# Linear attention and tanh-shrink MLP on one core: w_out's third quarter ahead of v, kv of batch 1 three slots later, first tiles of chunk 1 by head pairs

## The chip, the cores and the metric

The kernel runs on one core of one Trainium2 chip. The metric is device time in microseconds (us), the median of several executions. The kernel before takes 295.09 us (three runs, 294.81 to 295.49). The times of a kernel differ between chips and between executions by some tenths of a microsecond.

## The reference

```python
q_p, k_p = phi(q), phi(k)                    # phi(x) = exp(x) if x <= 0, else x + 1; 8 batches, 8 heads, 576 x 64
kv  = einsum('bhsd,bhse->bhde', k_p, v)
z   = sum(k_p, axis=2)
num = einsum('bhsd,bhde->bhse', q_p, kv)
den = einsum('bhsd,bhd->bhs', q_p, z)[..., None] + 1e-06
x   = (num / den) as [4608 tokens, 512]      # heads side by side
h   = x @ w_in                               # 512 -> 2048
out = (h - tanh(h)) @ w_out                  # 2048 -> 512
```

## The kernel before

The tokens are worked off in nine chunks of 512. Each chunk has a first layer of 16 tiles of four matmuls (one for each pair of heads; line 366), a tanh on ScalarE (372), a subtraction on VectorE into gT (373), and a second layer of 64 matmuls (387) in 16 slots of four. The attention of the later batches is tucked in between: lists s1 (behind tiles of the first layer) and s2 (behind slots of the second) say what is issued where. In the timelines here each engine takes its instructions in program order, so these lists also fix the order on VectorE and ScalarE.

In chunk 0 the second layer runs by quarters of w_out: slots 0 to 3 use the first quarter, 4 to 7 the second, 8 to 11 the third, 12 to 15 the fourth. Batch 1 is prepared there:

```python
def a_kv(b, banks):      # kv and z of a batch, masked into kz by VectorE (L177, L186)
def a_den(b, banks):     # denominators (L276), + 1e-6 (L281), reciprocal (L285)
def num1():              # numerators (L317, L320), copied out of PSUM by ScalarE (L344, L346)
def a_split(b):          # the reciprocal as a sum of bf16 numbers, w (L295 to L298)
def spread1(h):          # w spread over the partitions by matmuls (L354), two scales into xT (L359)

load_v(1)                # before: v of batch 1, then the third and fourth quarter of w_out
load_wo(2)
load_wo(3)
...
s2[7].append(lambda: (a_qT_pe(1, 0, side), a_qT_pe(1, 1, side), a_kv(1, side)))
s2[8].append(lambda: b0_scale_rest(side))
s2[9].append(lambda: a_den(1, side))
s2[10].append(lambda: (num1(), a_split(1)))
s2[11].append(lambda: spread1(0))
s2[12].append(lambda: q2(0))                    # exp and ramp of the first half of q of batch 2
s2[13].append(lambda: (spread1(1), q2(1)))      # exp and ramp of the second half
s2[14].append(lambda: q2(2))                    # both minima, then the transpose by DMA
s2[15].append(lambda: a_kphi(2, 0))
```

phi of a half batch is three instructions: exp on ScalarE (L134), the ramp max(x, 0) + 1 on VectorE (L135), and the minimum of both on VectorE (L136).

From batch 2 on the reciprocals take another way: from VectorE to DRAM (ds, L305), and back as a broadcast to all partitions (rdb, L308). Numerator products (L328) read rdb and free the two PSUM banks in which the numerators are made in turn. The loads of the batch after next are issued when the transposed q of the next batch is there:

```python
s1[0].append(lambda: (gate(qT_t[n1]), load_k(n2), load_q(n2), load_v(n2)))
s1[10 if c == 1 else 8].append(lambda: (a_den(n1, attn), a_spread(n1)))
...
if c == 1:
    s1[1].append(lambda: a_kphi(2, 1))
    for i in range(2):
        s1[3].append(lambda i=i: a_vp(2, i))    # v of batch 2 copied beside its column of ones, VectorE, L189
```

## Time and profile before

| engine | busy us | share of 293.2 us |
|---|---|---|
| TensorE | 285.2 | 97% |
| VectorE | 174.6 | 60% |
| ScalarE | 139.6 | 48% |

The main lines are shown in the prediction below. This is VectorE's timeline of the kernel before, around the start of chunk 1 (start, duration, engine, line, operation, sizes, number, and in brackets the idle time before it and what ended it):

```profile
51.02 0.45 DVE L135 TENSOR_SCALAR r<-qraw 128x1152 bf16<-128x1152 bf16 x1
51.39 1.42 DVE L136 TENSOR_TENSOR qp<-e,r 128x1152 bf16<-128x1152 bf16 x2
...
54.73 1.23 DVE L373 TENSOR_TENSOR gT<-ps_all,th 128x1024 bf16<-128x1024 f32 x1 [0.15 <-ACT th L372]
...
57.10 1.22 DVE L373 TENSOR_TENSOR gT<-ps_all,th 128x1024 bf16<-128x1024 f32 x1
58.23 0.82 DVE L189 COPY vp<-v 128x1152 bf16<-128x1152 bf16 x2
```

VectorE is nearly full here. In 51 to 62 us it is busy for 10.10 of 11 us, although it is busy for only 60% of the whole span.

### The profile page before, as it was taken

How to read it: one execution, taken by the hardware profiler on the slowest of the kernel's cores; microseconds unless marked ns; L12 is line 12 of the kernel's file. 1: busy time of each engine (PE TensorE's matmuls, PEld its weight loads, DVE VectorE, ACT ScalarE, POOL GpSimd, SP SyncE). 2: the span in 40 equal slices, each digit the busy share in tenths (PEclk: the TensorE clock that was granted, in tenths of full speed). 3: DMA queues.
4: the chain of work that ended last, by engine and by line, in shares of the span. 5: the costliest groups of instructions: out<-in, count | busy, mean ns of one | idle time of the engine just before them, and what ended most of it. 6: DMA issues, size and time to landing. Idle time of an engine off the chain costs nothing.

```text
span 293.2 us, 4504 instructions
## 1 busy us (share of the span) xinstructions
PE 285.2 (97%) x1801; PEld 134.3 (46%) x1801; DVE 174.6 (60%) x265; ACT 139.6 (48%) x168; POOL 33.3 (11%) x55
## 2 busy tenths in 40 slices
PE   8899999999999999999999999999999999999994
PEld 2544453454444444444444445444444444444443
DVE  4759857887567764786478646865581456106600
ACT  4938536947344643455246524661552155126411
POOL 8673030030030003000300020000000000000000
PEclk9999999999999999999999999999999999999999
DMA  6999999998999758955895669667117310131032
GB/s 101 194 204 212 208 207 216 200 145 153 234 163 185 160 118 139 218 117 129 136 223 127 139 134 183 134 154 143 38 24 178 73 36 0 38 84 24 0 74 72
DMA packets 39077, 38.94 MB, mean 133 GB/s; under 512 B 16336, under 2 KB 33808, under 8 KB 38288
## 3 DMA queue, kind: packets, MB, share of 16 engines
q0 software_dynamic: 17552, 18.35, 38.6%
q1 hardware_dynamic: 21344, 20.17, 30.3%
q8 instruction: 14, 0.23, 0.3%
q10 hardware_dynamic: 160, 0.13, 0.1%
q14 instruction: 7, 0.06, 0.1%
HBM read 43.91 MB, written 9.55 MB: 182 GB/s over the span
## 4 chain that ended last, share of the span: by engine, by line
PE 79%; DMA 11%; issue 7%; POOL 2%; DVE 0%; ACT 0%; POOLq 0%
PE ps_all L387 37%; PE ps_all L366 36%; DMA qraw<-in_q_dram 6%; DMA w_in_sb<-in_moe_w_in_dram 3%; PE ps_all L199 2%; DMA kraw<-in_k_dram 2%; PE ps_all L317 2%; PE ps_all L604 1%; PE ps_all L276 1%; POOL qraw L90 0%; ACT e L134 0%; POOL kraw L93 0%; DVE qp L136 0%; POOL v L93 0%; POOL w_out_sb L115 0%
## 5 line engine op out<-in xcount | busy, mean ns | idle before, releaser
L366 PE MATMUL ps_all<-xT,w_in_sb 128*128 128x512 bf16 x576 | 128.0, 379 | 0.3 <-DVE xT L244 0.3
L387 PE MATMUL ps_all<-w_out_sb,gT 128*128 128x512 bf16 x560 | 127.8, 379 | 0.0
L373 DVE TENSOR_TENSOR gT<-ps_all,th 128x1024 bf16<-128x1024 f32 x64 | 77.9, 1218 | 59.8 <-ACT th L372 59.8
L372 ACT ACTIVATE th<-ps_all 128x1024 f32<-128x1024 f32 x64 | 65.5, 1024 | 57.0 <-PE ps_all L366 47.1
L366 PEld LDWEIGHTS <-w_in_sb 128*128 128x128 bf16 x576 | 55.3, 98 | 66.6 <-issue 0.6
L387 PEld LDWEIGHTS <-gT 128*128 128x128 bf16 x560 | 54.1, 98 | 64.3 <-issue 0.3
L396 ACT COPY osb<-ps_all 128x512 f32<-128x512 f32 (+1 forms) x36 | 20.9, 583 | 73.4 <-PE ps_all L387 54.2
L328 DVE TENSOR_TENSOR xT<-ps_all,rdb 128x512 bf16<-128x512 f32 x24 | 16.3, 689 | 13.4 <-PE ps_all L317 11.2
L134 ACT ACTIVATE e<-qraw 128x1152 bf16<-128x1152 bf16 x16 | 18.5, 1162 | 6.9 <-DMA qraw<-in_q_dram 6.9
L134 ACT ACTIVATE e<-kraw 128x1152 bf16<-128x1152 bf16 x15 | 17.5, 1166 | 0.2 <-DMA kraw<-in_k_dram 0.2
L136 DVE TENSOR_TENSOR qp<-e,r 128x1152 bf16<-128x1152 bf16 x16 | 12.0, 757 | 7.8 <-ACT e L134 7.2
L136 DVE TENSOR_TENSOR kp<-e,r 128x1152 bf16<-128x1152 bf16 x15 | 11.4, 759 | 8.3 <-ACT e L134 7.5
L383 POOL COPY g<-qT 1x1 bf16<-1x1 bf16 x5 | 1.2, 240 | 120.6 <-DMA qT<-qp 120.6
L378 DVE TENSOR_TENSOR gT<-ps_all,th 128x512 bf16<-128x512 f32 x16 | 10.3, 685 | 2.4 <-ACT th L377 1.7
L377 ACT ACTIVATE th<-ps_all 128x512 f32<-128x512 f32 x16 | 9.2, 598 | 4.3 <-PE ps_all L366 3.1
L317 PE MATMUL ps_all<-qT,kz 128*128 128x512 bf16 x28 | 10.1, 379 | 0.0
L444 PE MATMUL ps_all<-zero 128*128 128x512 bf16 x29 | 8.8, 463 | 1.2 <-DVE zero L405 1.2
L135 DVE TENSOR_SCALAR r<-qraw 128x1152 bf16<-128x1152 bf16 x16 | 7.3, 453 | 2.2 <-DMA qraw<-in_q_dram 2.2
L199 PE MATMUL ps_all<-vp,kp 64*128 64x136 bf16 x216 | 7.4, 220 | 0.4 <-POOL g L383 0.4
L199 PEld LDWEIGHTS <-kp 64*128 64x128 bf16 x216 | 6.4, 94 | 3.0 <-issue 2.1
L285 DVE RECIPROCAL rden<-den 128x144 f32<-128x144 f32 x7 | 7.4, 1053 | 0.2
L394 DVE COPY osb<-ps_all 128x128 f32<-128x128 f32 x1 | 0.3, 292 | 11.6 <-PE ps_all L604 11.6
(82 smaller groups left out, 121.7 us busy)
## 6 DMA issues: line engine op xcount, KB each, us to landing
out_dram<-osb SPq DMA_DIRECT2D x70, 128.0 KB
rdb<-ds SPq DMA_DIRECT2D x12, 576.0 KB
kraw<-in_k_dram POOLq DMA_DIRECT2D x7, 576.0 KB, 7.1
qraw<-in_q_dram POOLq DMA_DIRECT2D x7, 576.0 KB, 9.0
v<-in_v_dram POOLq DMA_DIRECT2D x7, 576.0 KB, 12.2
w_out_sb<-in_moe_w_out_dram POOLq DMA_DIRECT2D x4, 512.0 KB, 16.4
w_in_sb<-in_moe_w_in_dram POOLq DMA_DIRECT2D x6, 256.0 KB, 8.6
qraw<-in_q_dram POOLq DMA_DIRECT2D x2, 288.0 KB, 4.6
```

The lines of the kernel that those rows point to most:

```text
L134: return (lambda: nc.scalar.activation(e, x, AF.Exp), lambda: nc.vector.tensor_scalar(r, x, 0.0, 1.0, ALU.max, ALU.add), lambda: nc.vector ...
L136: lambda: nc.vector.tensor_tensor(y, e, r, ALU.min))
L199: nc.tensor.matmul(ps[hg][:, i, :], kp[r, i, j].rearrange("p h d -> p (h d)"), vp[r, i, j, :], start=(j == 0), stop=(j == J - 1))
L317: nc.tensor.matmul(ps, kz[:, p // 2, p % 2, 0:128], qT[:, p % 2, 0:8, p // 2, :], start=True, stop=True)
L328: nc.vector.tensor_mul(xT[:, p, S * b:S * b + 512].rearrange("p (j t c) -> p j t c", j=8, t=4), ps.rearrange("p j (t c) -> p j t c", t=4), ...
L366: nc.tensor.matmul(h, w_in_sb[:, 2 * (p % 2) + p // 2, fi * 128:(fi + 1) * 128], xT[:, p, c * 512:(c + 1) * 512], start=(n == 0), stop=(n ...
L372: nc.scalar.activation(th, h, AF.Tanh)
L373: nc.vector.tensor_sub(gT[:, fi:fi + 2, :], h, th)
L377: nc.scalar.activation(th, h, AF.Tanh)
L378: nc.vector.tensor_sub(gT[:, fi, :], h, th)
L387: nc.tensor.matmul(o, gT[:, fi, i * 128:(i + 1) * 128], w_out_sb[:, fi, :], start=(fi == 0), stop=(fi == NF - 1))
L396: nc.scalar.copy(osb[:, f0:f1], o[:, f0:f1])
```

## The change

The intent is to close three holes of TensorE, 2.1 us together. The transposes of batch 1 are pulled apart, so that the second pass need not wait for its q; kv goes to slot 10, and everything behind it follows closely; w_out's third quarter is loaded ahead of v, because its slot now comes before kv. The second spread ends up behind slot 15, directly ahead of chunk 1, so the first two tiles of chunk 1 take the pairs of heads that are ready first. phi of batch 2 is rearranged, and kv of batch 2 moves one tile back.

```diff
+    load_wo(2)
     load_v(1)
-    load_wo(2)
     load_wo(3)
...
-            s2[7].append(lambda: (a_qT_pe(1, 0, side), a_qT_pe(1, 1, side), a_kv(1, side)))
-            s2[8].append(lambda: b0_scale_rest(side))
-            s2[9].append(lambda: a_den(1, side))
-            s2[10].append(lambda: (num1(), a_split(1)))
-            s2[11].append(lambda: spread1(0))
... (q2 and its slots 12 to 15)
+            s2[7].append(lambda: a_qT_pe(1, 0, side))
+            s2[8].append(lambda: a_qT_pe(1, 1, side))
+            s2[10].append(lambda: (a_kv(1, side), b0_scale_rest(side)))
+            s2[11].append(lambda: (a_den(1, side), num1(), a_split(1)))
+            s2[13].append(lambda: spread1(0))
...
+            s2[12].append(lambda: exp2(qs, q_t, qp_t, "qp", 0))
+            s2[13].append(lambda: exp2(qs, q_t, qp_t, "qp", 1))
+            s2[14].append(lambda: exp2(ks, k_t, kp_t, "kp", 0))
+            s2[15].append(lambda: (spread1(1), rest2(qs[0]), rest2(qs[1]), a_qT_dma(2), rest2(ks[0])))
...
-            s1[7 if c == 1 else 5].append(lambda: a_kv_cols(n1, attn))
+            s1[8 if c == 1 else 5].append(lambda: a_kv_cols(n1, attn))
...
+            if c == 1 and fi == 1:
+                for two in (0, 2):
+                    for f, o in ((0, ps_all[:, dense.order[(dense.n - 2) % 6], :]), (1, h)):
+                        for p in (two, two + 1):
+                            l1mm(c, f, o, p, p)
+            elif c != 1 or fi > 1:
+                for p in range(NP):
+                    l1mm(c, fi, h, p, p)
```

exp2 issues the exp of a half, rest2 its ramp and its minimum.

More of the change, by code (lines that the diff above doesn't have):

```diff
@@ L525, with exp2, rest2 @@
             s2[0].append(prepare)
-            s2[7].append(lambda: (a_qT_pe(1, 0, side), a_qT_pe(1, 1, side), a_kv(1, side)))
-            s2[8].append(lambda: b0_scale_rest(side))
-            s2[9].append(lambda: a_den(1, side))
-            s2[10].append(lambda: (num1(), a_split(1)))
-            s2[11].append(lambda: spread1(0))
-            def q2(n):
-                if n == 0:
-                    sub["q"] = [phi_pieces(2, q_t, qp_t, "qp", i) for i in range(2)]
-                if n < 2:
-                    for f in sub["q"][n][:2]:
-                        f()
-                else:
-                    for x in sub["q"]:
-                        x[2]()
-                    a_qT_dma(2)
-            s2[12].append(lambda: q2(0))
-            s2[13].append(lambda: (spread1(1), q2(1)))
-            s2[14].append(lambda: q2(2))
-            s2[15].append(lambda: a_kphi(2, 0))
+            s2[7].append(lambda: a_qT_pe(1, 0, side))
[3 more added lines that the diff above has]
+            s2[13].append(lambda: spread1(0))
+            qs, ks = [], []
+            def exp2(pieces, src, store, name, i):
+                pieces.append(phi_pieces(2, src, store, name, i))
+                pieces[i][0]()
+            def rest2(f):
+                f[1]()
+                f[2]()
+            s2[12].append(lambda: exp2(qs, q_t, qp_t, "qp", 0))
+            s2[13].append(lambda: exp2(qs, q_t, qp_t, "qp", 1))
+            s2[14].append(lambda: exp2(ks, k_t, kp_t, "kp", 0))
+            s2[15].append(lambda: (spread1(1), rest2(qs[0]), rest2(qs[1]), a_qT_dma(2), rest2(ks[0])))
         elif n1 < B:
-            s1[7 if c == 1 else 5].append(lambda: a_kv_cols(n1, attn))
+            s1[8 if c == 1 else 5].append(lambda: a_kv_cols(n1, attn))
             s1[10 if c == 1 else 8].append(lambda: (a_den(n1, attn), a_spread(n1)))
@@ L553 @@
             s1[1].append(lambda: a_kphi(2, 1))
-            for i in range(2):
-                s1[3].append(lambda i=i: a_vp(2, i))
+            s1[3].append(lambda: (a_vp(2, 0), a_vp(2, 1)))
         if c >= 1 and n2 < B:
@@ L582 @@
             h = first() if c == 0 else dense()
-            for p in range(NP):
-                l1mm(c, fi, h, p, p)
+            if c == 1 and fi == 1:
[6 more added lines that the diff above has]
+                    l1mm(c, fi, h, p, p)
             if c == 0:
```

## The prediction

> **What bounds the kernel now.** I read the page's busy rows first, then the chain that ended last in order of time, then TensorE's timeline, and last the timelines of the other engines over 30 to 80 us.
>
> ```profile
> PE 285.2 (97%) x1801; PEld 134.3 (46%) x1801; DVE 174.6 (60%) x265; ACT 139.6 (48%) x168; POOL 33.3 (11%) x55
> DMA  6999999998999758955895669667117310131032
> ```
>
> TensorE is busy in 97% of the span, and the DMA row is full for the first third: the loads are the second limit there.
>
> ```profile
> 234.05 13.81 PE ps_all L366 x64
> 247.87 13.81 PE ps_all L387 x64
> ```
>
> The chain gives the rate of a full stream: 64 matmuls in 13.81 us, 0.2158 us each. From 80 us on TensorE's rows follow one another at this rate without gaps. So only lost time in the first chunk and around the first two stages can be won. TensorE's timeline shows it:
>
> ```profile
> 31.03 7.07 PE L387 MATMUL ps_all<-w_out_sb,gT 128*128 128x512 bf16 x32
> 37.94 0.68 PE L164 MATMUL ps_all<-ident,qp 128*128 128x128 bf16 x9
> 39.17 0.68 PE L164 MATMUL ps_all<-ident,qp 128*128 128x128 bf16 x9 [0.56 <-DVE qp L136]
> 39.78 1.66 PE L177 MATMUL ps_all<-v,kp 64*128 64x192 bf16 x36
> ...
> 47.26 0.31 PE L354 MATMUL ps_all<-w,sel 32*128 32x144 bf16 x8 [0.69 <-ACT ns L344]
> ...
> 51.30 7.07 PE L366 MATMUL ps_all<-xT,w_in_sb 128*128 128x512 bf16 x32
> 58.74 1.24 PE L199 MATMUL ps_all<-vp,kp 64*128 64x136 bf16 x36 [0.37 <-POOL g L383]
> ```
>
> There are three holes. Counted in starts (the previous start plus its matmuls times 0.2158) they are 0.7 us before the second transposes, which wait for qp of batch 1; 0.86 us before the first spread (the four L387 from 45.54 end at 46.40); and 0.53 us before the kv of batch 2 (51.30 + 32 x 0.2158 = 58.21). The last is put down to POOL, but VectorE's copies of v into vp ran from 58.23 to 59.05: VectorE is the real releaser. Together that is 2.1 us, 0.7% of the span. It is all that the change could win.
>
> **What the Trainium skill says.** "TensorE: Matmul & The Clock Gate", Back-to-back issue gap: an isolated gap of N/2.4 + 2.5 ns, 215.8 ns for 512 columns, and a sustained 131 ns. The trace shows 215.8 ns in full streams, so I count with that; 131 ns does not show here. "Perfetto Trace Analysis", Identifying Performance Opportunities: an optimization looks for gaps on the most contended engine and for what ends them, and the limiting engine can change over time. The trace agrees: TensorE limits from 80 us, VectorE has hardly a gap from 51 to 61 us. "PSUM — Partial Sum Buffer", the section on bank collisions: guard by bank, not address. That is why the spread waits for ScalarE's copies out of banks 4 to 7. "DMA: Bandwidth & Descriptors", Queues, rings and completion order: each DMA engine takes turns between queue rows by packets. The four small ds writes issued at 65.45 to 66.74 nevertheless let rdb start only at 70.65, when the v load of batch 3 landed (60.32 + 10.3); other chunks need about 1 us.
>
> **The change part by part.** It removes no arithmetic. By the order of instructions each engine has the same ones, in another order.
>
> *Loads.* Landing is issue plus landing time: q of batch 1 at 19.39 + 16.5 = 35.9, v at 22.28 + 16.5 = 38.8, third quarter of w_out at 23.01 + 18.3 = 41.3, fourth at 43.9. So w_out costs 2.5 us and v 2.9 us of a full DMA. Swapped: w_out 38.4, v 41.3, fourth as before.
>
> *TensorE to the end of chunk 0.* Slot 7 ends at 37.94 as before. Nine transposes, 0.5: 38.44; the w_out quarter lands just then (0 to 0.2 lost). Slot 8: 39.36. The second qp is ready at 39.11, so the second transposes do not wait: 39.86. Slots 9 and 10: 41.59, v is there. kv 1.59: 43.18; rest numerators 0.12 and slot 11: 44.16. VectorE makes kz until 43.18 + 1.06 = 44.24, so den starts at about 44.3 and num ends at 45.63. Slots 12 and 13: 47.36. w comes 2.74 + 0.48 us after den's start, as from 43.32 to 46.54 now: 47.52. So the spread starts at 47.6, and 0.86 lost becomes 0.2. Slots 14 and 15: second spread at 49.66, chunk 1 at 49.89 instead of 51.30: **1.4 us won so far**.
>
> *Chunk 1's first tiles.* The four matmuls of pairs 0 and 1 fill 0.86 us, to 50.75. VectorE's scales start 0.35 after the spread and take 0.67 and 0.75: pair 2 is ready at about 50.75, pair 3 at 51.45. So pair 3 costs 0.5 us; without the new order it would cost about 0.9.
>
> *VectorE pays next.* In the kernel before it did one ramp of q in its wait for the spread; now all four scales come first, then q, q, k. Starts are 0.55 from ramp to minimum and 0.68 on from it (29.13, 29.68, 30.36 in its timeline). From 51.35 three pairs take 3.69: the first subtraction of chunk 1 starts at 55.04 and ends at about 56.2 (before: 54.73). Its bank pair is needed by the seventh tile at 52.15 + 4 x 0.863 = 55.6: 0.6 lost. One more pair (1.23) puts the second subtraction at 57.42 to 58.65 (before it started at 57.10); the ninth tile wants that bank at 57.97: 0.7 lost. That tile ends at 59.56, vp is ready at 59.4, kv follows at 59.56 and ends at 60.73. The tenth tile starts at 60.73; now it starts at 59.91 + 0.863 = 60.77. The sum of the won 1.4 and the lost 0.5 + 0.6 + 0.7, with the 0.53 vp wait absorbed: **-0.05 us at this point**.
>
> *DMA.* The transpose of q of batch 2 now follows all eight output writes and the second minimum: 53.9 instead of 53.48. Its landing (58.27 now, 4.8 after) gates the loads of batch 3, whose end released ds and rdb:
>
> ```profile
> 79.10 1.29 DVE L328 TENSOR_TENSOR xT<-ps_all,rdb 128x512 bf16<-128x512 f32 x2 [2.26 <-DMA rdb<-ds]
> ```
>
> The third numerator of chunk 1, at 79.98, needs the bank that this line's first product frees at about 79.78: slack is only 0.2 us. If rdb comes 0.4 later, TensorE loses 0.2; TensorE could not pass this point more than 0.2 earlier unless rdb also came earlier. No such wait shows in later chunks.
>
> So the estimate is max(-0.05, 0.4 - 0.2) with the transpose perhaps a little quicker without writes behind it: about 0.0 to +0.2 us on the span.
>
> **Rivals.** (a) *The 1.4 us is kept.* For it: later chunks have slack, and VectorE is busy only 60% overall. Against it: VectorE's lack of gaps at 51 to 61 us and the rdb line. It would give about 293.7; half kept, 294.4. (b) *The loads bind.* Both new landings are within 0.3 us of need. If the w_out quarter or v came 0.7 us late, everything after it would slide: 295.8. (c) *The transpose, loads, ds, rdb chain slides by a us.* The DMA queues are full at 62 to 69 us: 295.9. (d) *A clock difference.* The granted clock is 0.998, and nothing in the change adds work: excluded.
>
> **Range and chances.** The median of 295.09 plus 0.0 to 0.2 gives 295.1. The low side is rival (a) half kept plus run spread (0.3 below the median), 294.2; the high side is (b) or (c), 295.9. Two per cent is 5.9 us; all holes together are 2.1, so faster by 2% is excluded by the working, and slower needs a stall of 6 us that nothing suggests.
>
> **What would show it.** The second transposes start without a wait near 39.4; the first spread near 47.6, waiting for w; chunk 1's first matmul near 49.9; waits of TensorE for VectorE in the first, seventh and ninth tiles of chunk 1, together 1.5 to 2 us; kv of batch 2 near 59.5; the first product with rdb near 79.1 to 79.5. I am wrong if the scales or ramps end earlier than I say (then more is kept), if the seventh and ninth tiles do not wait, if L387 waits for w_out near 38.4 by more than 0.3 us, or if rdb lands before 78.5.

## The result, and the profile after

The changed kernel took 295.5 us (median of four, 295.45 to 295.57) against 294.95 for the kernel before (four, 294.7 to 295.49; three of them are the runs named at the top). The ratio is 1.0016, with a 95% interval of 0.9999 to 1.0034: the same, since differences under 2% are called the same here. A ratio is the mean time of one kernel's runs over that of the other's, so it is not quite the ratio of the medians. A second job gave 295.16 against 295.06, ratio 1.0004 (0.9985 to 1.0024).

The page of the kernel after, the busy row and the DMA row:

```profile
PE 283.4 (96%) x1773; PEld 133.9 (46%) x1801; DVE 174.6 (59%) x265; ACT 139.4 (47%) x168; POOL 33.4 (11%) x55
DMA  6999999878989658945796669767107310131032
```

The lower busy time of TensorE is not real: 28 of 1801 matmul records are missing in this trace. Among the rows of chunk 1 below none is missing: 5 + 19 + 8 + 4 matmuls are nine tiles of four.

TensorE's timeline of the kernel after, from slot 7 of chunk 0:

```profile
38.19 0.67 PE L164 MATMUL ps_all<-ident,qp 128*128 128x128 bf16 x9
...
39.56 0.67 PE L164 MATMUL ps_all<-ident,qp 128*128 128x128 bf16 x9
...
47.85 0.30 PE L354 MATMUL ps_all<-w,sel 32*128 32x144 bf16 x8
...
50.15 1.30 PE L366 MATMUL ps_all<-xT,w_in_sb 128*128 128x512 bf16 x5
51.74 4.26 PE L366 MATMUL ps_all<-xT,w_in_sb 128*128 128x512 bf16 x19 [0.29 <-DVE xT L359]
56.58 1.89 PE L366 MATMUL ps_all<-xT,w_in_sb 128*128 128x512 bf16 x8 [0.57 <-DVE gT L373]
58.94 1.02 PE L366 MATMUL ps_all<-xT,w_in_sb 128*128 128x512 bf16 x4 [0.48 <-DVE gT L373]
59.90 1.24 PE L199 MATMUL ps_all<-vp,kp 64*128 64x136 bf16 x36
```

The three holes are closed but for 0.20 us at the first spread (45.92 + 8 x 0.2158 = 47.65, and it starts at 47.85), and three new ones are open. The first transposes already stand 0.25 us later than before (38.19 against 37.94). In eleven more profiles, in which TensorE has the same instructions up to there, they stood between 37.74 and 38.46, and the second profile of this same kernel has the 37.74. That is the spread of the opening, and I subtract it from here on. Chunk 1 starts at 50.15 instead of 51.30: 1.15 us earlier, 1.4 without the opening. Then TensorE waits for the fourth scale, at the seventh tile for the first subtraction and at the ninth for the second. Counted in starts, with 0.2158 us for a matmul, that is 51.74 - (50.15 + 5 x 0.2158) = 0.51, 56.58 - (51.74 + 19 x 0.2158) = 0.74 and 58.94 - (56.58 + 8 x 0.2158) = 0.63. Together 1.88 us were given back. The tenth tile starts when kv with its 1.17 us is through, at 59.90 + 1.17 = 61.07, which is 22.88 us after the first transposes; before it was 60.77, or 22.83.

VectorE's timeline of the kernel after shows who asked for it back:

```profile
50.27 1.42 DVE L359 TENSOR_TENSOR xT<-ns,ps_all 128x576 bf16<-128x576 f32 x2 [0.58 <-PE ps_all L354]
51.61 0.46 DVE L135 TENSOR_SCALAR r<-qraw 128x1152 bf16<-128x1152 bf16 x1
52.17 0.76 DVE L136 TENSOR_TENSOR qp<-e,r 128x1152 bf16<-128x1152 bf16 x1
...
55.31 1.22 DVE L373 TENSOR_TENSOR gT<-ps_all,th 128x1024 bf16<-128x1024 f32 x1
...
57.67 1.22 DVE L373 TENSOR_TENSOR gT<-ps_all,th 128x1024 bf16<-128x1024 f32 x1
```

After the second scale it sits idle for 0.58 us, and then has no gap that the view lists until the second subtraction. The subtractions come at 55.31 and 57.67 instead of 54.73 and 57.10, so tiles that are ready earlier find their banks still taken.

The second wall comes later. The chain that ended last, of the kernel after, in order of time (start, duration, what), has both:

```profile
55.39 1.15 DVE gT L373
...
66.75 4.31 DMA ds<-rden
...
71.71 7.90 DMA rdb<-ds
...
79.73 0.70 DVE xT L328
80.44 0.04 issue
80.48 0.38 PE ps_all L317
```

It runs through VectorE at the start of chunk 1, then through ds and rdb, and enters TensorE at the third numerator, at 80.48. This is TensorE's timeline of the kernel before at the same place:

```profile
78.95 1.03 PE L387 MATMUL ps_all<-w_out_sb,gT 128*128 128x512 bf16 x4
79.85 0.38 PE L317 MATMUL ps_all<-qT,kz 128*128 128x512 bf16 x1
```

The difference of 0.63 us (80.48 against 79.85) stays to the end: the last chunk's tail stands at 286.32 instead of 285.69. Without the opening it is 0.38 us; in the second profile of the changed kernel it is 0.24 (42.15 against 41.91 in the table below).

### The profile page after: what moved, and what is told of

It reads as the page before. It is cut to its first block, busy times and chain, and to the rows that moved or that the text cites. A ratio compares the mean times of both kernels' runs of the same rounds, so it can differ in the third digit from the quotient of the medians. Undisturbed runs are those within 1.5% of the kernel's fastest.

```text
span 293.8 us, 4475 instructions
## 1 busy us (share of the span) xinstructions
PE 283.4 (96%) x1773; PEld 133.9 (46%) x1801; DVE 174.6 (59%) x265; ACT 139.4 (47%) x168; POOL 33.4 (11%) x55
## 4 chain that ended last, share of the span: by engine, by line
PE 80%; DMA 9%; DVE 5%; ACT 2%; issue 1%; POOL 1%; SPq 1%; DVEq 0%; ACTq 0%; POOLq 0%
PE ps_all L366 37%; PE ps_all L387 35%; DMA rdb<-ds 3%; DMA v<-in_v_dram 2%; DMA out_dram<-osb 2%; PE ps_all L199 2%; PE ps_all L317 2%; DMA ds<-rden 1%; PE ps_all L276 1%; DVE gT L378 1%; DVE gT L373 1%; ACT th L377 1%; ACT osb L396 1%; PE ps_all L177 1%; DVE qp L136 1%
## 5 line engine op out<-in xcount | busy, mean ns | idle before, releaser
L387 PE MATMUL ps_all<-w_out_sb,gT 128*128 128x512 bf16 x547 | 126.0, 379 | 0.7
L328 DVE TENSOR_TENSOR xT<-ps_all,rdb 128x512 bf16<-128x512 f32 x24 | 16.3, 690 | 13.8 <-PE ps_all L317 11.2
```

The costliest lines, as they stand in the source:

```text
L328: nc.vector.tensor_mul(xT[:, p, S * b:S * b + 512].rearrange("p (j t c) -> p j t c", j=8, t=4), ps.rearrange("p j (t c) -> p j t c", t=4), ...
L387: nc.tensor.matmul(o, gT[:, fi, i * 128:(i + 1) * 128], w_out_sb[:, fi, :], start=(fi == 0), stop=(fi == NF - 1))
```

## The experiments

Times are from five rounds unless said otherwise. All experiments gave correct results. A kernel's runs are compared with the runs of the kernel before that the record lists with them; e5 to e10 and the second job ran on one chip and share eleven of these, e1 to e4 ran on another. The table has, from each profile, the start of the tenth tile of chunk 1, the start of the third numerator of chunk 1 and the end of the span, all counted from the first transposes of chunk 0 (us).

| kernel | median us | before, listed with it | ratio (95%) | tenth tile | third numerator | end |
|---|---|---|---|---|---|---|
| before | 295.09 | | | 22.83 | 41.91 | 255.3 |
| after | 295.5 | 294.95 | 1.0016 (0.9999-1.0034) | 22.88 | 42.29 | 255.6 |
| after, second job | 295.16 | 295.06 | 1.0004 (0.9985-1.0024) | 22.97 | 42.15 | 255.5 |
| e1_ramp | 295.12 | 294.91 | 1.0006 (0.9994-1.0019) | 22.31 | 41.79 | 255.1 |
| e2_vgate | 294.9 | 294.91 | 1.0002 (0.999-1.0015) | 22.87 | 41.92 | 255.2 |
| e3_ramp_vgate | 294.59 | 294.91 | 0.9989 (0.9976-1.0003) | 22.41 | 41.45 | 254.7 |
| e4_spread_dve | 293.97 | 294.91 | 0.9965 (0.9953-0.9978) | 21.68 | 40.72 | 254.0 |
| e9_spread_nogate | 294.49 | 295.12 | 0.998 (0.9962-0.9998) | 21.77 | 41.31 | 254.6 |
| e10_by_pair | 293.79 | 295.06 | 0.9955 (0.9937-0.9973) | 21.68 | 40.72 | 254.0 |
| e5_no_pairs | 295.28 | 295.12 | 1.0007 (0.9988-1.0025) | 22.88 | 42.46 | 255.7 |
| e8_kv7 | 295.46 | 295.12 | 1.0011 (0.9992-1.0029) | 23.25 | 42.54 | 255.9 |
| e6_loads_undone | 299.75 | 295.12 | 1.0157 (1.0136-1.0178) | 27.00 | 46.38 | 259.7 |
| e7_loads_only | 296.9 | 295.06 | 1.0063 (1.0043-1.0083) | 24.52 | 43.56 | 256.9 |

The theory is that two walls set the end: VectorE's queue at the start of chunk 1, and behind it the arrival of rdb. The rivals are that ScalarE or the banks cause the stalls, that there is only the first wall, and that ds is slow by itself and not through the loads.

**e1_ramp.** The first ramp of batch 2 goes into VectorE's gap of 0.58 us.

```diff
-            s2[13].append(lambda: exp2(qs, q_t, qp_t, "qp", 1))
+            s2[13].append(lambda: (exp2(qs, q_t, qp_t, "qp", 1), qs[0][1]()))
-            s2[15].append(lambda: (spread1(1), rest2(qs[0]), rest2(qs[1]), a_qT_dma(2), rest2(ks[0])))
+            s2[15].append(lambda: (spread1(1), qs[0][2](), rest2(qs[1]), a_qT_dma(2), rest2(ks[0])))
```

> The changed kernel, with the first ramp of q of batch 2 put into VectorE's gap of 0.58 us between the second and the third scale. Theory D+R (VectorE's queue sets when the seventh and ninth tile of chunk 1 start, and after that the arrival of rdb sets when the third numerator of chunk 1 starts): the first subtraction of chunk 1 starts near 54.8 instead of 55.31, kv of batch 2 near 59.35 instead of 59.90, so TensorE is 0.55 us ahead there; the transpose of q of batch 2 starts 0.38 earlier (53.85), rdb lands 0.4 earlier (79.3), and the third numerator moves only by that: 80.1 instead of 80.48. Time 295.1. Rival S (the stalls of chunk 1 come from ScalarE or from the banks, not from VectorE's order): no move, 295.5. Rival N (no second wall at rdb): 0.55 plus the 0.36 wait, 294.6.

TensorE's timeline of this run:

```profile
51.43 6.16 PE L366 MATMUL ps_all<-xT,w_in_sb 128*128 128x512 bf16 x27 [0.29 <-DVE xT L359]
58.06 1.02 PE L366 MATMUL ps_all<-xT,w_in_sb 128*128 128x512 bf16 x4 [0.48 <-DVE gT L373]
...
79.67 0.38 PE L317 MATMUL ps_all<-qT,kz 128*128 128x512 bf16 x1 [0.27 <-DVE xT L328]
```

The seventh tile's wait falls from 0.74 to 0.17 us by its starts, below what the view lists, and the tenth tile is 0.57 us earlier than in the changed kernel. One ramp on VectorE did that, so this stall was VectorE's order and not ScalarE or a shortage of banks. But the third numerator still waits for rdb (the bracket of the last line) and gained 0.50; the time is 295.12, as the theory with two walls had it (295.1), not 294.6. The five runs spread from 294.75 to 295.4, so the trace decides here more than the time.

**e2_vgate.** v of batch 3 is loaded only when the reciprocal of batch 2 is there. A one-element copy on GpSimd that reads the reciprocal holds the load back.

```diff
+    def gate_f(t):
+        g1 = rpool.tile([1, 1], F32, name="g1")
+        nc.gpsimd.tensor_copy(g1, t[0:1, 0:1])
...
+            if c == 1:
+                s1[0].append(lambda: (gate(qT_t[n1]), load_k(n2), load_q(n2)))
+                s1[10].append(lambda: (gate_f(rden_t[n1]), load_v(n2)))
+            else: ... (as before)
```

> The changed kernel, with the load of v of batch 3 held back until the reciprocal of batch 2 is done (near 65.7), so that it does not lie ahead of the small ds writes. Theory R (the ds writes, and so rdb, wait behind the loads of batch 3): ds lands near 68.5 instead of 71.1, rdb's first product starts before 78.4 (when its numerator is there) instead of 79.73, the third numerator no longer waits and starts near 80.15 instead of 80.48; kv of batch 2 stays at 59.9. Time 295.2. Rival L (the ds writes have a latency of 4 us of their own under load, whatever lies ahead): rdb no more than 0.3 earlier, and the time 295.4 to 295.5.

The lines are from the DMA queue's and VectorE's timelines of this run:

```profile
68.68 1.25 SPq L308 DMA_DIRECT2D rdb<-ds  x2
...
78.61 1.41 DVE L328 TENSOR_TENSOR xT<-ps_all,rdb 128x512 bf16<-128x512 f32 x2 [1.58 <-DMA rdb<-ds]
```

rdb is issued at 68.68 instead of 71.18, so the ds writes did wait for the loads ahead of them, and the rival with a latency of 4 us of its own falls. The 2.5 us shrink to 1.1 at the first product, most likely because v's load, issued at 66.19, now runs beside rdb; that product came 0.2 us later than I expected. It is early enough: the third numerator no longer waits, and the median is 294.9. In all four runs with this gate (e2, e3, e4, e10) rdb is issued 8.5 to 8.7 us after q's load of batch 3, although ds itself is issued 3.0 to 4.1 us ahead of rdb. That too is the picture of a ds that waits for the loads still ahead of it.

**e3_ramp_vgate.** Both edits together.

> Both of the edits before together. Theory D+R: kv of batch 2 near 59.35, no wait at the third numerator (near 79.6), so the sum is 0.55 + 0.36 = 0.9 us: 294.6, more than the two edits apart add up to (0.4 + 0.3). Rival N (rdb is no wall): the gains of the two just add.

Measured: 294.59, no wait at the third numerator. The sum came out as expected. The finer claim, that both together give more than the sum, is not shown: against 295.5, from another job, the two edits alone gave 0.4 and 0.6 and both gave 0.9. The time of e2 was better than the 295.2 expected, and a spread of 0.3 us hides the rest.

**e4_spread_dve.** In addition, the second ramp and minimum of k go behind the second subtraction, and the copies of v to ScalarE.

```diff
-            s1[1].append(lambda: a_kphi(2, 1))
-            s1[3].append(lambda: (a_vp(2, 0), a_vp(2, 1)))
+            k1 = []
+            s1[1].append(lambda: (k1.extend(phi_pieces(2, k_t, kp_t, "kp", 1)), k1[0]()))
+            s1[3].append(lambda: (k1[1](), k1[2](), a_vp(2, 0, True), a_vp(2, 1, True)))   # True: on ScalarE
```

> As before, and the second ramp and minimum of k of batch 2 behind the second subtraction of chunk 1, with the copies of v of batch 2 on ScalarE instead of VectorE. Theory D+R: neither the seventh nor the ninth tile waits more than 0.1 us; kv of batch 2 near 58.7, 1.2 us ahead of the changed kernel; the third numerator near 79.0 unless rdb lands after 78.3; time 293.9 to 294.2. Rival S (ScalarE, with 2.2 us more work there, becomes the bound): the tanh of tiles 5 and 6 comes 1 us late, the eleventh tile waits, and the gain over the third edit is below 0.2 us.

TensorE's timeline of this run:

```profile
51.55 7.02 PE L366 MATMUL ps_all<-xT,w_in_sb 128*128 128x512 bf16 x31 [0.29 <-DVE xT L359]
58.51 1.24 PE L199 MATMUL ps_all<-vp,kp 64*128 64x136 bf16 x36
```

From the fourth scale to kv the view lists no wait, and no record is missing (5 + 31 matmuls are nine tiles). By the starts 0.27 us are left, 58.51 - (51.55 + 31 x 0.2158): 0.17 of it at the seventh tile, a little more than the 0.1 expected. The tenth tile is 1.20 us ahead of the changed kernel, and the time is 293.97, with the whole interval below the kernel before. ScalarE had room for 2.2 us of copies, so the rival that it becomes the bound falls.

**e9_spread_nogate.** e4 without the gate: the same VectorE, but ds behind the loads.

> The fourth edit without the gate on the load of v of batch 3. VectorE no longer holds up TensorE before kv of batch 2 (58.5), but rdb comes as in the first edit. Theory R: the first product with rdb starts near 78.9 and the third numerator waits for it, near 79.65 instead of 78.72, so the time is that of the first edit, 294.9 to 295.1, although 0.5 us more of stalls are gone. Rival N (no wall at rdb): 294.0 as with the gate.

```profile
79.42 0.38 PE L317 MATMUL ps_all<-qT,kz 128*128 128x512 bf16 x1 [0.34 <-DVE xT L328]
```

The wait for rdb is back in TensorE's timeline, although the tenth tile is within 0.1 us of e4's. So the gate alone is worth 0.6 us at the third numerator (41.31 against 40.72) and 0.5 in the median (294.49, 293.97; two chips). The wall is there, and 294.0 without one is refuted. The number I expected (294.9 to 295.1) was missed by 0.4 us: rdb's first product started at 78.7, 0.5 us earlier from the first transposes than in e1. So this wall does not stand still. Why it moved is open; the transpose began 0.1 later than in e1 on that count, and ds was issued 0.5 earlier, so it is not the time of the loads alone that sets it.

**e5_no_pairs.** The first two tiles of chunk 1 in plain order.

```diff
-            if c == 1 and fi == 1:
+            if False:
...
-            elif c != 1 or fi > 1:
+            else:
```

> The changed kernel with the first two tiles of chunk 1 in the plain order again (all four pairs of the first, then of the second). Theory D (VectorE's queue sets the seventh tile): the first tile ends 0.43 us later, the second ends at 52.8 instead of 52.4, but the seventh tile still starts with the end of the first subtraction, near 56.5, so its wait shrinks from 0.57 to 0.15-0.25 and kv of batch 2 stays at 59.9; time 295.4 to 295.6. Rival H (the order by pairs is worth its 0.43 us): kv at 60.3 and 295.9.

Measured: 295.28, and the tenth tile at 22.88, exactly that of the changed kernel. The first tile now waits for the third scale too, and the seventh waits less. The order by pairs does bring the second tile 0.4 us forward, but these 0.4 us are lost again at VectorE's queue.

**e8_kv7.** kv of batch 2 behind the eighth tile again.

```diff
-            s1[8 if c == 1 else 5].append(lambda: a_kv_cols(n1, attn))
+            s1[7 if c == 1 else 5].append(lambda: a_kv_cols(n1, attn))
```

> The changed kernel with kv of batch 2 behind the eighth tile of chunk 1 again instead of the ninth. Theory D: kv then waits for VectorE's copies of v (0.7 to 0.9 us, start near 59.1) and the ninth tile no longer waits for the second subtraction; both are done near 61.1 either way, time 295.4 to 295.6. Rival K (the later slot is worth the 0.5 us that kv waited in the kernel before): 296.0.

```profile
59.12 1.24 PE L199 MATMUL ps_all<-vp,kp 64*128 64x136 bf16 x36 [0.85 <-POOL g L383]
```

As expected kv waits for the copies of v (VectorE's, whatever the bracket says). I had expected both slots to be through at the same time (near 61.1). That was missed: the tenth tile is 0.3 to 0.4 us later than in the changed kernel, so the later slot has some use there; the time of 295.46 doesn't show it.

**e6_loads_undone.** v ahead of w_out's third quarter again, all else as changed (three rounds).

```diff
-    load_wo(2)
     load_v(1)
+    load_wo(2)
```

> The changed kernel with v of batch 1 ahead of the third quarter of w_out again, as before the change. If the swap is what makes the moved kv possible, slot 8 waits for that quarter until 41.3: its first matmul comes 2.7 us later than 38.6, everything behind it slides by about as much, chunk 1 starts near 52.7 and the time is 297.8 to 298.2. Rival: the loads were hidden anyway, 295.5.

TensorE's timeline of this run, and then a row of the windows view (window, length, busy us and number of TensorE, of its weight loads, VectorE, ScalarE, GpSimd; granted clock; DMA share, GB/s):

```profile
41.34 1.17 PE L387 MATMUL ps_all<-w_out_sb,gT 128*128 128x512 bf16 x4 [2.30 <-DMA w_out_sb<-in_moe_w_out_dram]
...
43.26 3.00 PE L387 MATMUL ps_all<-w_out_sb,gT 128*128 128x512 bf16 x8
```

```profile
42.00:45.50 3.50, 3.50 (x17) 1.88 (x16) 0.42 (x1) 0.69 (x1) 0.00 (x0) 0.51 1.22 208
```

TensorE waited until 41.34, as computed: 41.34 - (38.38 + 0.5) = 2.46 us. But the time is 299.75, 1.6 us above the range. From 42.09 to 45.50 the granted clock was one half (the windows view gives 0.50 there, and 1.00 before and behind); eight matmuls took 3.00 us instead of 1.89. From the first transposes to kv 7.82 us passed, against 3.69 in the changed kernel: 4.13 us lost, of which 2.46 are the wait and 1.67 the clock. My expectation left the clock out. The swap of the loads is thus necessary for the new order, and worth more than the wait it avoids.

**e7_loads_only.** The swap alone, in the kernel before.

```diff
+    load_wo(2)
     load_v(1)
-    load_wo(2)
```

> The kernel before with the swap of the two loads alone. kv of batch 1 stays in slot 7 and wants v at 39.8; v now lands near 41.3, so TensorE waits 1.5 us there and everything behind it slides: 296.2 to 296.6 if the granted clock stays whole. If the idle time lowers the clock for 3.4 us, as the 2.3 us wait for w_out did in the run with the loads undone, 1 us or more comes on top: 297.5. Rival (the loads were hidden): 295.0.

```profile
41.56 1.66 PE L177 MATMUL ps_all<-v,kp 64*128 64x192 bf16 x36 [1.61 <-DMA v<-in_v_dram]
```

kv waits 1.61 us for v and the time is 296.9, a little above the range for a whole clock. The profiled run (296.69) had the clock whole. The slowest of the six, 297.92, had a mean granted clock of 0.994; four of four in e6 had 0.993 or 0.994. So a wait of 2.5 us went with a low clock each time. Whether a wait of 1.6 us can cost the clock is not shown by one run of six, since a low clock also comes without such a wait: one of the twelve runs of the kernel before that are listed here had 0.993 and took 296.44, which widens the intervals of this job.

**e10_by_pair.** e4, and pair 2 of both first tiles before pair 3 of both.

```diff
-                    for f, o in ((0, ps_all[:, dense.order[(dense.n - 2) % 6], :]), (1, h)):
-                        for p in (two, two + 1):
+                    for p in (two, two + 1):
+                        for f, o in ((0, ps_all[:, dense.order[(dense.n - 2) % 6], :]), (1, h)):
```

> The fourth edit (ramp in the gap, v gated, VectorE's work spread), with the second half of the first two tiles in another order: pair 2 of both, then pair 3 of both. Pair 3 then comes one matmul (0.22 us) later and its wait for the fourth scale falls from 0.5 to 0.3 us. VectorE's first subtraction (54.55 to 55.7) still has to be there for the seventh tile, which now starts near 55.5 at the earliest: so 0.0 to 0.2 us less than the fourth edit, 293.8 to 294.0, and 1.5 us less than the changed kernel on the same chip.

```profile
55.82 2.75 PE L366 MATMUL ps_all<-xT,w_in_sb 128*128 128x512 bf16 x12 [0.23 <-DVE gT L373]
```

The wait at pair 3 falls below what the view lists (by the starts from 0.44 in e4 to 0.23), and the seventh tile waits longer instead (0.38 instead of 0.17). The tenth tile stays at 21.68. The median is 293.79, against 293.97 for e4 on another chip, which shows no difference. It is the best version: 1.37 us below the changed kernel in the same job (293.79, 295.16), and 0.45% below the kernel before by the ratio.

**after_again.** The changed kernel once more, in the last job.

> The changed kernel unedited, on the same chip as the next two, to compare them directly and to see how far its own runs spread: 295.2 to 295.6, the kernel before 294.9 to 295.1.

Measured: 295.16 (294.92 to 295.69). The medians of the two jobs (295.5, 295.16) lie 0.34 us apart, so the excess over the kernel before (0.55 and 0.10 by medians) is not shown to be above zero by the times alone.

The part with den and numerators directly behind kv can't be undone by itself: with kv in slot 10 the old spacing would need slots beyond 15. It stays untested alone.

## Why the prediction was right or wrong

The prediction of 295.1 with a range of 294.2 to 295.9 was right, and mostly by its own steps. The number alone says little: a forecast that nothing changes would lie in that range too. What counts is that the steps can be checked one by one.

- *Loads and slots of chunk 0:* right. The second transposes ran without a wait (39.56, predicted 39.4 and 0.25 of opening), the first spread at 47.85 (47.6), chunk 1 at 50.15 (49.9). e6 and e7 show that both landings were needed as computed.
- *The gain of 1.4 us by then:* right, 1.15 + 0.25.
- *What the first tiles give back:* predicted 0.5, 0.6 and 0.7, measured 0.51, 0.74 and 0.63. The tenth tile was predicted 0.05 us earlier than before and came 0.05 later. (The rounded terms of the prediction add up to 0.14 earlier; its starts, 60.73 against 60.77, give the 0.05.) e1 and e4 show that the last two came from VectorE's queue.
- *The worth of the order by pairs:* "without the new order it would cost about 0.9" holds for that place, but e5 shows that the end doesn't see it. The text did not say so.
- *The transpose and rdb:* the transpose was to start 0.42 later and started 0.50 later (54.23 - 53.48 - 0.25); rdb was to be 0.4 later and its first product was 0.38 later, 0.25 in the second profile. ds itself was issued only 0.06 later (65.76 - 65.45 - 0.25), so the delay arose behind its issue. e2 and e9 show that the loads ahead of ds hold it back. But the prediction's reading that the landing of v releases ds does not hold: in the changed kernel v landed at 72.17 (60.97 + 11.2), 1 us after rdb was issued at 71.18. In the kernel before the two fell together (70.62 and 70.65), and the prediction took that for the cause. That the later transpose alone made rdb later was not tested, and e9 speaks for a share of ds's own time.
- *The slack at the third numerator:* this step was mis-sized. "Slack is only 0.2 us" was read from a start of 79.98 in the chain of waits. That view begins a piece where the one before ends. TensorE's timeline has the start at 79.85, 78.95 + 4 x 0.2158 = 79.81 is where it could have been, and in the changed kernel the matmul starts 0.75 after the product does, so 79.10 + 0.75 = 79.85. The slack was nothing. The loss was therefore the whole delay of rdb, 0.38 us (0.24 in the second profile), and not 0.2. That is about half of the 0.4 us by which the point estimate was too low in the first job; in the second job it was 0.06 too low.
- *The rival with half of the gain kept* did not come true, but e4 shows how it could have: its order of VectorE's work and its gate on v keep 1.15 of the 1.4 us at the tenth tile (21.68 against 22.83).

## What to carry to other kernels

When TensorE is pulled forward at one place, look at the engine that frees its banks: even if that engine is idle for 40% of the span, it may have no gap in the stretch that matters, and its order there is worth as much as TensorE's. Then look for the next arrival behind it, here a small write to DRAM that waits behind big loads. A chain of waits tells the order of things; take exact starts for a slack of a few tenths from the timeline.

## What the Trainium skill lacked or had wrong

- "TensorE: Matmul & The Clock Gate", Part 1 (the HAM clock gate), gives a window of about 3.4 us, free-running, and as abstract rule no idle gaps above about 3.4 us. Here, in the profile of e6, the granted clock was one half from 42.09 to 45.50 after a gap of 2.46 us that ended at 41.34, and that cost 1.67 us; all four runs of e6 had a mean clock of 0.993 or 0.994. The two levels and the length of the throttled stretch agree with the page; as a rule the 3.4 us are too generous for this case.
- The same page's 131 ns for sustained matmuls of 512 columns was not seen in any trace here; 215.8 ns, its isolated gap, held in the full streams.
- "VectorE: DVE Perf Modes", The DRAIN you can't avoid, reports for eight copies that a semaphore after each costs nothing extra. It has no figure for an operation that waits for the one directly ahead of it. In the kernel before, a ramp is followed by a minimum that does not need it after 0.37 us (51.02, 51.39); in the kernel after, by the minimum that does need it after 0.56 us (51.61, 52.17). Three such pairs are part of what VectorE's queue cost.
- "DMA: Bandwidth & Descriptors", Queues, rings and completion order, has turns by packets between queue rows, but no figure for what a small hardware-queue write waits behind a full software queue. Here ds took 4.31 us from its last issue to its landing behind three loads, and rdb could be issued 2.5 us earlier when the third of them was held back.
